# Even frequency classes of a real DFT transformed by row parity over half the columns, and the second batch's class sums moved into layer 1

## The chip, the cores and the metric

The kernel runs on one core of one Trainium2 chip. The metric is the device time of one execution in microseconds, the median of three runs. TensorE does the matrix products into PSUM, VectorE (DVE), ScalarE (ACT) and GpSimd (POOL) work elementwise, and SyncE (SP) issues most of the DMA transfers. Each engine runs its own instructions strictly in the order in which the program emits them.

## What is computed

```python
def _attn_ref(x):                      # x: 2 x 3008 x 256, float32
    X = np.fft.fft(x, axis=1)
    X = np.fft.fft(X, axis=2)
    return X.real.astype(np.float32)

def _moe_ref(x, w_in, w_out):          # 6016 tokens, 256 -> 2048 -> 256
    h = x @ w_in
    g = np.where(h >= 1, h, np.where(h <= -1, 0.0, (h + 1) ** 2 / 4.0))
    return g @ w_out

def _moe2_ref(x, w_in, w_out):
    h = x @ w_in
    g = np.maximum(0.01 * h, h)
    return g @ w_out
```

The second layer's input is the first layer's output, whose input is the real part of the two-dimensional transform.

## The kernel before

The rows of the sequence are folded by their symmetries, so that each batch becomes four classes of frequencies of 376 positions: class 0 holds the frequencies 4i (378 columns with its two ends), class 1 holds 4i + 2, and classes 2 and 3 hold the odd ones. With two batches these are eight units, u = 4b + class. A folded batch comes in three chunks of 126 rows: chunk 0 has the even rows, chunk 1 the odd rows, and chunk 2 has 63 even rows on partitions 0 to 62 and 62 odd ones on partitions 64 to 125.

The head prepares all that layer 1 needs. `load_x`, `load_q`, `sum_x` and `add_x` bring and add the source terms, `fold_x b c` (VectorE) folds a chunk, and `col_copy` sets one column of it aside. `even_product b j c` multiplies chunk c by a cosine and a sine matrix (`me`, loaded by `load_me`), each over 378 or 376 columns, into two PSUM banks. `odd_product b tr c` uses parity: the even rows go to one bank and the odd rows to another (`parts`), ScalarE copies one bank out (`odd_copy`), and VectorE forms the sum and the difference of the two (`odd_sum`). Every class is then split into a high half in the reduced format fp32r (`even_high`, `odd_high`, ScalarE) and a low remainder (`even_low`, `odd_low`, VectorE; with `_g` on GpSimd), which land in `bt[u]`. The column set aside is transformed by `col_even` and spread over the partitions by `col_even_out` (ScalarE) into `ct[0]`, `ct[1]`, `ct[4]`, `ct[5]`; the odd units' `ct` go out to DRAM as a row and come back spread over all partitions (`col_row`, SP's queue). The transform over the 256 features is folded into the first weights: `w1_begin`, `w1_exponent` and `w1_join` turn the 64-bit weights to float32, `g_product j` multiplies them by the feature transform, `g_high` and `g_low` split the result. `w2_*` do the same conversion for the second weights. `fill` issues matmuls on a constant tile whose result is not used.

Layer 1 has 128 steps, n = 16u + f, one for each unit and each block of 128 hidden features. A step's first product is 6 matmuls into a pair of banks `p` (high by high, high by low, low by high for two parts), VectorE makes `aa` from `ct`, `g128` and `p` and then the two `h`, ScalarE makes `r` in three instructions, VectorE takes the maximum in the next step, two steps later ScalarE writes the high half `gh` and GpSimd the low half `gl`, and four steps later (`LAG`) TensorE accumulates into four banks `acc` with 12 matmuls. Pairs of banks are double-buffered, so step n + 2 waits for `h` of step n. The single banks (four) serve `g_product`, `col_even`, some of the class products and, until `g_last 1`, the bank `g128`; from step 4 on they are `acc`.

The order of the head is written out by hand in `ORDER`: each engine takes its part of the items in that order. Work that has time is planned into the steps: `plan_at(step, (offset, kind, function))` puts a job behind a step. Steps 0 and 1 stand in `ORDER`, the later ones in a loop. Layer 2 follows with another 128 steps. The tail of the order before:

```python
# open_steps, odd_low 1 0, step 0, g_rows 1, odd_product 1 1 0, w2_join 3, even_low 1 1, odd_product 1 1 1,
# odd_product 1 1 2, w2_high 3, w2_high 1, odd_copy 1 1, w2_high 2, w2_low_g 3, w2_low_g 1, odd_sum 1 1,
# w2_low_g 2, g_last 1, w2_high 0, odd_high 1 1, odd_low_g 1 1, step 1, col_row 1, w2_low 0
```

Of the kernel before, what the change touches and what calls it, by code (L numbers as in the profile page):

```python
# [60 lines left out]

def _dft_even():

    s = _rows().astype(np.float64)[:, :, None]
    ok = s >= 0
    i = np.arange(378)[None, None, :]
# [66 lines left out]
1, odd_product 0 0 1, odd_product 0 1 1, g_product 4, load_me 2, w1_join 3, g_product 3, sum_x 0 2, fold_x 0
2, g_low 2, g_high 4, g_high 3, w1_begin 0, fill 1, odd_product 0 0 2, g_low 3, col_copy 0 2, load_w1 6,
even_product 0 1 0, even_product 0 1 1, load_x 1 1, w1_begin 6, g_row 3, load_me 0, g_low 4, odd_product 0 1
2, w1_exponent 0, odd_copy 0 0, add_x 1 1, w1_begin 5, load_me 1, fold_x 1 0, load_x 1 2, w1_join 0,
w1_exponent 6, even_product 0 1 2, even_product 0 0 0, g_product 0, odd_copy 0 1, odd_sum 0 0, even_product
0 0 1, g_row 2, odd_sum 0 1, even_product 0 0 2, w1_exponent 5, w1_join 5, even_high 0 1, load_w2 0,
even_low 0 1, load_w2 1, w1_join 6, even_high 0 0, w2_begin 1, fold_x 1 1, col_copy 1 0, odd_product 1 0 0,
load_w1 7, g_product 5, g_product 6, g_high 6, load_w2 2, odd_product 1 0 1, even_low 0 0, add_x 1 2,  # L140
load_w2 3, fold_x 1 2, even_product 1 0 0, col_row 0, g_high 0, w1_begin 7, col_copy 1 2, g_low 0, odd_high
0 0, w2_begin 0, even_product 1 0 1, w1_exponent 7, col_copy 1 1, g_row 4, w1_join 7, w2_exponent 1,
odd_product 1 0 2, g_product 7, load_w2 4, g_row 0, even_product 1 0 2, w2_join 1, odd_copy 1 0, odd_sum 1
0, w2_begin 2, g_high 5, odd_low_g 0 0, even_high 1 0, even_product 1 1 0, w2_exponent 0, g_rows 0, w2_join
0, g_high 7, even_product 1 1 1, odd_high 0 1, w2_begin 3, g_low 5, odd_low 0 1, g_low 6, g_low 7,
w2_exponent 2, w2_join 2, col_even 1, w2_exponent 3, even_low 1 0, g_row 7, even_product 1 1 2, g_last 0,
col_even 0, odd_high 1 0, g_row 5, col_even_out 1, even_high 1 1, g_row 6, col_even_out 0, open_steps,
# [8 lines left out]
def fnet_moe_kernel(ctx: ExitStack, tc: tile.TileContext, xpq, dft_e, dft_o, dft_d, pick,  # L156
# [146 lines left out]
    wpb = t5 = ta = th = None  # L303

    with tc.manual_schedule():
# [5 lines left out]
        ev = pool("ev", 4, late, "right")  # L311
# [11 lines left out]
        col = mo_p.tile([CH, 3, 2, B, P // B], F32, name="col")  # L323
# [22 lines left out]
        def load_me(j):  # L346
            me[j] = me_p.tile([P, 3, 378], F32, name=f"me{j}")
# [85 lines left out]
        def col_copy(b, c):  # L433
# [4 lines left out]
            A.copy(col[:, c, :, b, :], tc_[:, 0:2, P:P + 1].to_broadcast([CH, 2, P // B]))  # L438

        def both(c, j, lo=0, hi=CH):  # L440
            return col[lo:hi, c, j].rearrange("p b r -> p (b r)")

        def new_unit(u):
            bt[u] = by.tile([P, 4, 378], FR, tag="by", name=f"bt{u}")

        def even_parts(b, j):
            u = 4 * b + j
            n = 378 if j == 0 else H4
            return [(bt[u][:m, 2 * i, :n], bt[u][:m, 2 * i + 1, :n], p[:m, :n])
                    for i, (m, p) in enumerate(zip((P, 127), pde[b, j]))]  # L450

        def even_product(b, j, c):

            n = 378 if j == 0 else H4
            if c == 0:
                new_unit(4 * b + j)
                if (b, j) == (0, 1):
                    pde[b, j] = (psum_one(f"dc{b}{j}"), psum_one(f"ds{b}{j}"))
                else:
                    p = psum_pair(f"de{b}{j}")  # L460
                    pde[b, j] = (p[:, 0], p[:, 1])
            pc, pn = pde[b, j]
            tc_, ts_ = xt[b, c]
            T.matmul(pc[:, :n], lhsT=tc_[:, j, 0:P], rhs=me[2 * j][:CH, c, :n], start=(c == 0), stop=(c == 2))  # L464
            T.matmul(pn[:127, :n], lhsT=ts_[:, j, 0:127], rhs=me[2 * j + 1][:CH, c, :n], start=(c == 0), stop=(c == 2))

        def even_high(b, j):
            for hi, _, p in even_parts(b, j):
                A.copy(hi, p)

        def even_low(b, j):
            for hi, lo, p in even_parts(b, j):
                V.tensor_tensor(out=lo, in0=p, in1=hi.bitcast(F32), op=ALU.subtract)

        def col_even(j):
            n = 378 if j == 0 else H4
            pde["c", j] = p = psum_one(f"cc{j}")
            for c in range(3):
                T.matmul(p[:, :n], lhsT=both(c, j), rhs=me[2 * j][:CH, c, :n], start=(c == 0), stop=(c == 2))  # L479

        def col_spread(b, u, src):

            n = 378 if u == 0 else H4
            ct[4 * b + u] = t = cp.tile([P, 378], F32, tag="ct", name=f"ct{4 * b + u}")
            for h in range(2):
                A.copy(t[64 * h:64 * h + 64, :n], src[64 * b:64 * b + 64, :n])

# [447 lines left out]
```

## Time and profile before

| | |
|---|---|
| median of three runs (lowest to highest) | 981.23 us (980.51 to 981.66) |
| the profiled execution's own time | 983.23 us |
| its span in the profile | 978.4 us |
| TensorE, matmuls | 963.2 us busy, 5442 records |
| VectorE | 603.9 us |
| ScalarE | 707.9 us |
| GpSimd | 492.1 us |

The span is what the profiler records from the first to the last instruction; the execution's time holds also what lies around it. A matrix product in full float32 leaves two matmul records, one in fp32r leaves one. Busy times are those of one profiled execution; matmuls are pipelined, so the distance from one start to the next says more than a record's own duration.

### The profile page before, as it was taken

To read this page: it belongs to the slowest core of one execution; us is meant where nothing else is said; L and a number is where in the kernel's file an instruction comes from. 1 tells how busy PE (TensorE), PEld (TensorE's weight loads), DVE (VectorE), ACT (ScalarE), POOL (GpSimd) and SP (SyncE) were. 2 spreads that over 40 slices of the span, in tenths; PEclk is the share of its full clock that TensorE was granted. 3 is DMA by queue.
4 is the path that set the end of the run, shared out by engine and by line. 5 is a ranking of instruction groups with operands and counts; after the bars stand their busy time and mean duration, and the time that the engine had idled before them with its cause. 6 is when DMAs were issued, how large, how long until landed. Compare 5 with 4: busy or idle time off the path is not lost.

```text
span 978.4 us, 14606 instructions
## 1 busy us (share of the span) xinstructions
PE 963.2 (98%) x5442; PEld 937.0 (96%) x5442; DVE 603.9 (62%) x1005; ACT 707.9 (72%) x1236; POOL 492.1 (50%) x293
## 2 busy tenths in 40 slices
PE   8998999999999999999999999999999999999998
PEld 6558999999999999999999999999999999999998
DVE  6989988888798888887766473342433524325211
ACT  3488988878798888888766676666666666666654
POOL 0145655556556565656320455645646446465443
PEclk9998999999999999999999999999999999999999
DMA  9822010111010101011453210101001010000000
GB/s 353 295 68 74 1 54 12 54 43 54 12 54 33 64 12 54 11 65 44 141 203 119 85 44 16 48 1 64 1 16 49 1 64 1 1 32 1 33 1 31
DMA packets 19838, 56.47 MB, mean 58 GB/s; under 512 B 2564, under 2 KB 3128, under 8 KB 19640
## 3 DMA queue, kind: packets, MB, share of 16 engines
q1 hardware_dynamic: 18872, 53.56, 15.2%
q0 software_dynamic: 752, 1.61, 0.8%
q8 instruction: 42, 0.69, 0.3%
q10 hardware_dynamic: 144, 0.39, 0.1%
q14 instruction: 28, 0.23, 0.1%
HBM read 37.95 MB, written 14.44 MB: 54 GB/s over the span
## 4 chain that ended last, share of the span: by engine, by line
PE 91%; DVE 2%; ACT 2%; POOL 0%; issue 0%; ACTq 0%; DVEq 0%
PE acc L606 53%; PE p L589 13%; PE x L595 12%; PE v L595 6%; PE q L776 3%; PE y L595 3%; ACT gh L611 0%; PE do L499 0%; PE cc L479 0%; DVE aa L734 0%; ACT r L740 0%; ACT r L751 0%; DVE h L737 0%; DVE r L747 0%; PE de L464 0%; POOL gl L615 0%
## 5 line engine op out<-in xcount | busy, mean ns | idle before, releaser
L615 POOL TENSOR_TENSOR gl<-s,gh 128x752 fp32r<-128x752 f32 x113 | 205.6, 1820 | 240.1 <-ACT gh L611 239.3
L615 POOL TENSOR_TENSOR gl<-r,gh 128x752 fp32r<-128x752 f32 x128 | 239.2, 1869 | 164.7 <-ACT gh L611 136.8
L606 PE MATMUL acc<-gh,wd 128*128 128x376 f32 x1024 | 288.0, 334 | 0.4 <-DVE o L636 0.4
L606 PE MATMUL acc<-gh,wb 128*128 128x376 f32 x1024 | 282.2, 336 | 0.2
L606 PEld LDWEIGHTS acc<-gh,wb 128*128 128x128 f32 x1024 | 187.0, 189 | 3.3 <-ACT r L744 2.3
L606 PEld LDWEIGHTS acc<-gh,wd 128*128 128x128 f32 x1024 | 186.8, 188 | 0.7 <-DVE o L636 0.7
L606 PE MATMUL acc<-gl,wb 128*128 128x376 f32 x512 | 171.3, 335 | 1.2 <-POOL gl L615 1.2
L606 PE MATMUL acc<-gl,wd 128*128 128x376 f32 x512 | 170.1, 332 | 0.0
L589 PE MATMUL p<-bt,wa 127*128 127x376 f32 (+3 forms) x768 | 154.9, 337 | 4.5 <-DVE h L738 4.5
L763 ACT ACTIVATE s<-s 128x752 f32<-128x752 f32 x112 | 75.7, 676 | 94.2 <-DVE s L840 94.2
L589 PEld LDWEIGHTS p<-bt,wa 128*128 128x128 f32 (+1 forms) x768 | 135.4, 190 | 5.3 <-issue 5.1
L747 DVE TENSOR_TENSOR r<-h,r 128x752 f32<-128x752 f32 x128 | 125.6, 981 | 0.0
L830 DVE TENSOR_TENSOR s<-v,bb 128x376 f32<-128x376 f32 x56 | 30.8, 550 | 152.0 <-PE v L595 133.7
L611 ACT CAST gh<-s 128x752 fp32r<-128x752 f32 x128 | 105.2, 822 | 15.6 <-PE acc L606 10.9
L751 ACT ACTIVATE r<-r 128x752 f32<-128x752 f32 x128 | 106.8, 834 | 4.1
L740 ACT ACTIVATE r<-h 128x376 f32<-128x376 f32 x128 | 66.2, 517 | 59.7 <-DVE h L737 54.9
L734 DVE SCALAR_TENSOR_TENSOR aa<-ct,g,p 128x376 f32<-128x376 f32 (+1 forms) x128 | 77.3, 604 | 50.4 <-PE p L589 48.8
L611 ACT CAST gh<-r 128x752 fp32r<-128x752 f32 x128 | 103.3, 807 | 0.2 <-DVE r L747 0.2
L606 PEld LDWEIGHTS acc<-gl,wb 128*128 128x128 f32 x512 | 96.8, 189 | 2.3 <-POOL gl L615 2.3
L606 PEld LDWEIGHTS acc<-gl,wd 128*128 128x128 f32 x512 | 96.1, 188 | 0.0
L595 PE MATMUL x<-op,ws 128*128 128x376 f32 x336 | 76.0, 334 | 0.0
L595 PE MATMUL v<-op,ws 128*128 128x376 f32 x336 | 75.6, 333 | 0.0
(105 smaller groups left out, 1264.3 us busy)
## 6 DMA issues: line engine op xcount, KB each, us to landing
rw<-in_w_dram SPq DMA_DIRECT2D x32, 512.0 KB, 5.4
y<-o SPq DMA_DIRECT2D x16, 376.0 KB, 2.6
ry<-y SPq DMA_DIRECT2D x16, 376.0 KB, 3.6
out_dram<-o SPq DMA_DIRECT2D x15, 376.0 KB, 2.5
rf<-w3f SPq DMA_DIRECT2D x16, 256.0 KB, 2.7
x<-in_xpq_dram SPq DMA_DIRECT2D x6, 512.0 KB, 8.6
wt<-wc SPq DMA_DIRECT2D x8, 384.0 KB, 5.2
me<-in_dft_e_dram SPq DMA_DIRECT2D x4, 567.0 KB, 11.3
```

The costliest lines, as they stand in the source:

```text
L589: T.matmul(p[:, j, :n], lhsT=w[:m, 2 * j + x, :], rhs=b[:m, 2 * j + y, :n], start=(a == 0), stop=(a == 2))
L595: T.matmul(bank[:, :H4], lhsT=w[:, x, :], rhs=y[:, z, :], start=start and a == 0, stop=a == 2, skip_group_check=not start)
L606: T.matmul(acc[k][:, :H4], lhsT=w[:, x, m * P:(m + 1) * P], rhs=y[:, t, :], start=(f == 0 and i == 0), stop=(f == NF - 1 and i == 2))
L611: A.copy(gh[n], gp[n])
L615: engine.tensor_tensor(out=gl[n], in0=gp.pop(n), in1=gh[n].bitcast(F32), op=ALU.subtract)
L734: V.scalar_tensor_tensor(out=aa[:, :w], in0=ct[u][:, :w], scalar=g128[:, f:f + 1], in1=p[:, 0, :w], op0=ALU.mult, op1=ALU.add)
L740: A.activation(r[:, 0], h[:, 0], HOLD, scale=240.0)
L747: V.tensor_tensor(out=g, in0=hp.pop(n - 1), in1=g, op=ALU.max)
L751: A.activation(r, r, AF.Square, scale=0.5 / 240.0, bias=0.5)
L763: A.activation(out, h, AF.Prelu, alpha=0.01)
L776: T.matmul(p[:, t, :H4], lhsT=block[:, x, :], rhs=ops[0][d][:, t, z, :], start=(a == 0), stop=(a == 5))
L830: V.tensor_tensor(out=h1[:, 1], in0=v[:, :H4], in1=bb, op=ALU.add)
```

## The change

The even classes are transformed by parity like the odd ones. The matrices keep 192 columns instead of 378. `halves` sends even rows to one bank and odd rows to the other, cosine and sine part side by side in a bank; `even_copy` takes the even rows' bank out, and the sum and the difference of the two (`even_plus`, `even_minus`, 189 or 188 columns) give the two halves of the columns, which now lie in another order (`_even_columns`, undone on the host). The high and low halves are then taken from SBUF instead of PSUM. For batch 1, both banks of the even and of the odd classes are copied ("parked") into a tile, and sums, highs and lows are done by planned jobs in steps 18 to 58. The column set aside is transformed as one row a batch, its halves are combined on two partitions (`even_row`, `even_row_sum`), and it goes out to DRAM and comes back spread over the partitions (`even_row_out`, SP's queue). Steps 0 to 3 now stand in `ORDER`, whose items are put in a new order; the planned jobs of steps 0 to 3 are emitted behind it.

```diff
-        col = mo_p.tile([CH, 3, 2, B, P // B], F32, name="col")
+        col = mo_p.tile([CH, 3, 2, B], F32, name="col")
...
-            me[j] = me_p.tile([P, 3, 378], F32, name=f"me{j}")
+            me[j] = me_p.tile([P, 3, HW], F32, name=f"me{j}")
...
-            A.copy(col[:, c, :, b, :], tc_[:, 0:2, P:P + 1].to_broadcast([CH, 2, P // B]))
+            A.copy(col[:, c, :, b], tc_[:, 0:2, P])
...
+        parts = (((0, 0, CH),), ((1, 0, CH),), ((0, 0, 63), (1, 64, CH)))
+
+        def halves(banks, i, m, lhs, mat, c):
+            for par, lo, hi in parts[c]:
+                T.matmul(banks[par][:m, i * HW:(i + 1) * HW], lhsT=lhs(lo, hi), rhs=mat[lo:hi, c, :],
+                         start=(c == par and i == 0), stop=(c == 2), skip_group_check=(i > 0))
...
-            pc, pn = pde[b, j]
-            tc_, ts_ = xt[b, c]
-            T.matmul(pc[:, :n], lhsT=tc_[:, j, 0:P], rhs=me[2 * j][:CH, c, :n], start=(c == 0), stop=(c == 2))
-            T.matmul(pn[:127, :n], lhsT=ts_[:, j, 0:127], rhs=me[2 * j + 1][:CH, c, :n], start=(c == 0), stop=(c == 2))
+                pde[b, j] = two_banks(f"de{b}{j}", (b, j) == (0, 1))
+            for i, (x, m) in enumerate(zip(xt[b, c], (P, 127))):
+                halves(pde[b, j], i, m, lambda lo, hi: x[lo:hi, j, 0:m], me[2 * j + i], c)
+
+        def even_copy(b, j):
+            t = park("even")[:, 2 * j:2 * j + 2] if b else first_part(b, f"e{j}")
+            for i, m in enumerate((P, 127)):
+                for par in range(1 + b):
+                    A.copy(t[:m, i, par * HW:(par + 1) * HW], pde[b, j][par][:m, i * HW:(i + 1) * HW])
...
+        def even_plus(b, j, i):
+            m, e, o = sum_parts(b, j, i)
+            a = 189 - j
+            V.tensor_tensor(out=sum_tile(4 * b + j, i)[:m, :a], in0=o[:, :a], in1=e[:, :a], op=ALU.add)
+
+        def even_minus(b, j, i):
+            m, e, o = sum_parts(b, j, i)
+            a, k = 189 - j, 2 - 2 * j
+            x, y = (o, e) if i else (e, o)
+            V.tensor_tensor(out=ss[4 * b + j, i][:m, a:2 * a], in0=x[:, k:k + a], in1=y[:, k:k + a],
+                            op=ALU.subtract)
...
-            for h in range(2):
-                A.copy(t[64 * h:64 * h + 64, :n], src[64 * b:64 * b + 64, :n])
...
+            A.copy(e, p[0][:B, :HW])
+
+            def rest():
+                V.tensor_tensor(out=d[:, :a], in0=p[1][:B, :a], in1=e[:, :a], op=ALU.add)
+                V.tensor_tensor(out=d[:, a:z], in0=e[:, lo:hi], in1=p[1][:B, lo:hi], op=ALU.subtract)
...
+            nc.sync.dma_start(out=row[:, :z], in_=d[:, :z])
             for b in range(B):
...
+                nc.sync.dma_start(out=t[:, :z], in_=row[b:b + 1, :z].to_broadcast([P, z]))
...
         def odd_copy(b, tr):
-            pdo[b, tr] = sums_of_odd(f"{b}{tr}", pdo[b, tr], P)
+
+            if b:
+                for h in range(2):
+                    A.copy(park("odd")[:, 2 * tr + h, :H4], pdo[b, tr][h][:, :H4])
+            else:
+                A.copy(first_part(b, f"o{tr}").rearrange("p i n -> p (i n)")[:, :H4], pdo[b, tr][0][:, :H4])
...
+        at = 18
+        for u in (4, 5):
+            for i in range(2):
+                n, m = (378, H4)[u - 4], (P, 127)[i]
+                plan_at(at, (0, "V", lambda u=u, i=i: even_plus(1, u - 4, i)),
+                        (2, "V", lambda u=u, i=i: even_minus(1, u - 4, i)),
+                        (3, "A", lambda u=u, i=i, m=m, n=n: high_of(u, i, m, n)),
+                        (4, "V", lambda u=u, i=i, m=m, n=n: low_of(u, i, m, n)))
+                at += 6
+        for tr in range(2):
+            m = (P, 127)[tr]
+            plan_at(at, (0, "V", lambda tr=tr: odd_plus(1, tr)), (2, "V", lambda tr=tr: odd_minus(1, tr)))
+            if tr:
+                plan_at(at, (4, "S", lambda: col_row(1)))
+            for h in range(2):
+                plan_at(at, (3 + h, "A", lambda h=h, tr=tr, m=m: high_of(6 + h, tr, m, H4)),
+                        (5 + 2 * h, "V", lambda h=h, tr=tr, m=m: low_of(6 + h, tr, m, H4)))
+            at += 10
...
-            if 1 < n < N1 + 2:
+            if first_steps <= n < N1 + 2:
```

The weight tiles `wpb` are in two pools of four instead of one of eight, and the pool `t3` of `gh` and `gl` is opened by `open_steps`. The new order from the last fold on:

```python
# fold_x 1 2, odd_product 1 0 1, load_w2 2, even_product 1 0 2, g_low 5, w1_begin 7, col_copy 1 1, col_copy 1 2,
# odd_high 0 1, col_even 1, g_low 6, odd_product 1 0 2, w1_exponent 7, load_w2 0, w1_join 7, col_even 0, even_row 1,
# even_product 1 1 0, g_product 7, odd_product 1 1 0, even_row_sum 1, even_row_out 1, odd_copy 1 0, w2_begin 3,
# w2_join 1, even_low_g 0 1, g_low 0, even_row 0, g_row 0, even_product 1 1 1, w2_exponent 3, w2_begin 2, g_row 2,
# g_high 7, w2_begin 0, even_product 1 1 2, even_row_sum 0, w2_join 3, even_copy 1 0, even_low 0 0,
# odd_product 1 1 1, g_low 7, w2_exponent 2, odd_product 1 1 2, even_row_out 0, g_rows 0, w2_join 2, w2_exponent 0,
# g_row 5, open_steps, w2_high 3, w2_join 0, w2_high 1, w2_high 2, odd_low 0 0, g_row 7, g_row 6, w2_low_g 2,
# odd_low 0 1, g_last 0, load_w2 4, even_copy 1 1, w2_low 1, g_rows 1, w2_high 0, odd_copy 1 1, col_row 0, step 0,
# step 1, w2_low_g 0, step 2, step 3, g_last 1, w2_low 3
```

## Rows read from the trace of the kernel before

**Rows 1.** The page, part 1: busy time, share of the span and instructions of each engine.

```profile
PE 963.2 (98%) x5442; PEld 937.0 (96%) x5442; DVE 603.9 (62%) x1005; ACT 707.9 (72%) x1236; POOL 492.1 (50%) x293
```

**Rows 2.** Stretches: us, busy of PE, PEld, DVE, ACT, POOL, PEclk, DMA share, GB/s.

```profile
5.79:48.70 42.91, 40.98 (x162) 28.55 (x161) 38.15 (x94) 19.52 (x51) 4.99 (x7) 1.00 0.94 337
48.70:64.14 15.44, 14.86 (x56) 9.09 (x55) 12.92 (x27) 12.70 (x32) 4.91 (x8) 1.00 0.30 95
...
70.00:80.00 10.00, 5.28 (x20) 4.21 (x19) 9.90 (x17) 7.94 (x15) 6.21 (x6) 0.72 0.52 185
98.00:148.00 50.00, 49.95 (x290) 49.52 (x289) 45.07 (x74) 44.09 (x74) 30.24 (x16) 1.00 0.08 27
148.00:198.00 50.00, 49.98 (x290) 49.53 (x289) 41.38 (x69) 41.59 (x69) 29.48 (x16) 1.00 0.09 32
```

**Rows 3.** Timeline of TensorE in the head: start us, us, instruction, records.

```profile
31.49 1.54 PE L499 MATMUL do<-mo,xt 63*128 63x376 f32 x8
32.97 0.90 PE L464 MATMUL dc<-me,xt 126*128 126x376 f32 x2
...
36.44 1.89 PE L372 MATMUL g<-cw,cd 128*128 128x256 f32 x8
38.16 0.80 PE L464 MATMUL de<-me,xt 126*128 126x378 f32 x2
38.80 0.80 PE L465 MATMUL de<-me,xt 126*127 126x378 f32 x2
```

**Rows 4.** The chain that ended last, in order of time: start us, us, what.

```profile
57.41 1.90 PE cc L479 x6
...
62.99 1.05 PE p L589 x6
64.04 4.04 PE do L499 x16
...
68.10 0.62 ACT wb L293
...
68.74 0.48 ACT es L516
...
70.32 0.53 DVE aa L734
...
73.33 1.38 DVE wb L297
...
77.15 2.00 POOL gl L615
...
79.19 3.06 PE acc L606 x11
```

**Rows 5.** Timeline of VectorE in the head: start us, us, instruction, idle before.

```profile
27.14 2.07 DVE L395 TENSOR_TENSOR wa<-g,wa 128x256 fp32r<-128x256 f32 x6
...
48.70 0.75 DVE L395 TENSOR_TENSOR wa<-g,wa 128x256 fp32r<-128x256 f32 x2
...
50.48 2.33 DVE L216 TENSOR_SCALAR tw<-tw 128x512 int32<-128x512 int32 x1
...
59.48 0.42 DVE L216 TENSOR_SCALAR tw<-tw 128x512 int32<-128x512 int32 x1
59.93 0.69 DVE L221 SCALAR_TENSOR_TENSOR cw<-rw,tw 128x512 int32<-128x512 int32 x1
...
64.14 0.61 DVE L734 SCALAR_TENSOR_TENSOR aa<-ct,g,p 128x378 f32<-128x378 f32 x1 [1.28 <-ACT ct L486]
```

**Rows 6.** Timeline of GpSimd beside the stretched shift.

```profile
50.57 1.94 POOL L543 TENSOR_TENSOR bt<-bs,bt 128x376 fp32r<-128x376 f32 x2
```

**Rows 7.** Timeline of SP's queue: a row written out and read back.

```profile
51.02 0.33 SPq L556 DMA_DIRECT2D row<-bs  x1
53.96 0.35 SPq L558 DMA_DIRECT2D ct<-row  x1
```

**Rows 8.** Groups of VectorE's instructions from 98 to 498 us: busy us, mean ns.

```profile
L747 DVE TENSOR_TENSOR r<-h,r 128x752 f32<-128x752 f32 x120 | 116.8, 974 | 0.0
```

More of the change, by code (lines that the diff above doesn't have):

```diff
@@ L133 @@
[L133 to L147, printed above, removed]
@@ L148 @@
-odd_low 1 0, step 0, g_rows 1, odd_product 1 1 0, w2_join 3, even_low 1 1, odd_product 1 1 1, odd_product 1
-1 2, w2_high 3, w2_high 1, odd_copy 1 1, w2_high 2, w2_low_g 3, w2_low_g 1, odd_sum 1 1, w2_low_g 2, g_last
-1, w2_high 0, odd_high 1 1, odd_low_g 1 1, step 1, col_row 1, w2_low 0
+load_q 0 0, load_x 0 0, load_w1 2, w1_begin 2, load_w1 1, sum_x 0 0, load_x 0 2, load_cd, w1_begin 1, load_q
+0 2, fold_x 0 0, load_w1 4, load_w1 3, load_q 0 1, w1_begin 3, load_w1 0, w1_exponent 2, w1_exponent 1,
@@ new lines @@
+even_product 0 1 0, g_low 3, g_high 4, load_w1 5, odd_product 0 1 1, fold_x 1 0, g_low 1, load_x 1 2,
+even_product 0 1 1, add_x 1 2, w1_begin 5, w1_exponent 6, odd_product 0 1 2, w1_join 6, load_me 0, g_low 4,
+w1_exponent 5, odd_copy 0 0, load_w2 1, load_w2 3, even_product 0 1 2, odd_sum 0 0, even_copy 0 1, w1_join
+0, g_row 3, g_row 1, g_product 6, col_copy 1 0, even_sum 0 1, even_product 0 0 0, odd_high 0 0, odd_copy 0
+1, w2_begin 1, even_product 0 0 1, even_product 0 0 2, fold_x 1 1, even_high 0 1, load_w1 7, g_product 0,
@@ new lines @@
+w1_join 5, g_product 5, even_copy 0 0, w2_exponent 1, g_high 0, g_high 5, odd_sum 0 1, even_sum 0 0, g_row
+4, odd_product 1 0 0, g_high 6, even_high 0 0, even_product 1 0 0, even_product 1 0 1, fold_x 1 2,
+odd_product 1 0 1, load_w2 2, even_product 1 0 2, g_low 5, w1_begin 7, col_copy 1 1, col_copy 1 2, odd_high
+0 1, col_even 1, g_low 6, odd_product 1 0 2, w1_exponent 7, load_w2 0, w1_join 7, col_even 0, even_row 1,
+even_product 1 1 0, g_product 7, odd_product 1 1 0, even_row_sum 1, even_row_out 1, odd_copy 1 0, w2_begin
@@ new lines @@
+3, w2_join 1, even_low_g 0 1, g_low 0, even_row 0, g_row 0, even_product 1 1 1, w2_exponent 3, w2_begin 2,
+g_row 2, g_high 7, w2_begin 0, even_product 1 1 2, even_row_sum 0, w2_join 3, even_copy 1 0, even_low 0 0,
+odd_product 1 1 1, g_low 7, w2_exponent 2, odd_product 1 1 2, even_row_out 0, g_rows 0, w2_join 2,
+w2_exponent 0, g_row 5, open_steps, w2_high 3, w2_join 0, w2_high 1, w2_high 2, odd_low 0 0, g_row 7, g_row
+6, w2_low_g 2, odd_low 0 1, g_last 0, load_w2 4, even_copy 1 1, w2_low 1, g_rows 1, w2_high 0, odd_copy 1 1,
@@ L151 @@
+col_row 0, step 0, step 1, w2_low_g 0, step 2, step 3, g_last 1, w2_low 3
 """.replace("\n", " ").split(",")]
@@ L852, in layer_2_pair @@
             todo(n + 1, "V")
+        first_steps = sum(item.startswith("step") for item in ORDER)
         for item in ORDER:
             name, *args = item.split()
[L856 removed]
+            if name == "w2_high" and not wpb:
                 folded.close()
[L858 removed]
+                wpb.append(pool("wpb0", 4))
             if name == "step":
```

190 lines of the change are left out of this document (109 added, 81 removed).

## The prediction

> **What bounds the kernel now.** I read the page's engine shares first: TensorE is busy for 963 of the 978 us [rows 1], so a gain needs TensorE work taken away or its idle time filled. The table by stretches says where either is possible: from 98 us on it is busy without a gap [rows 2], and the change takes nothing away there. What can move is the head, up to the first accumulation of layer 1 at 79.19 us, from where the chain of waits stays on TensorE [rows 4]. In the head two engines are near full. Between 5.79 and 48.70 us TensorE shows 40.98 of 42.91 us and VectorE 38.15; between 48.70 and 64.14 TensorE shows 14.86 of 15.44 [rows 2], and the chain lies on it: column product, first step, odd product [rows 4]. The ramp of the pipeline behind that is VectorE's: 9.90 of 10 us in 70:80, with TensorE at 5.28 [rows 2].
>
> **What TensorE loses.** An even product now has 6 matmuls of 376 or 378 columns. Each is two records and takes 0.64 us (38.16 to 38.80 [rows 3]), 3.82 for one class of a batch. After: 4 matmuls over all rows of a chunk and 4 over half of them, 192 columns each. Eight 256-column records take 1.72 us (36.44 to 38.16 [rows 3]), 0.215 each, and a 378-column one 0.32: time goes with the columns, so 0.161 for 192, at most 0.215 if the proportion ends below 256. Eight full-row records: 1.29 (to 1.72). The half-row form stands in the odd product: eight 63-row records of 376 columns take 1.48 us (31.49 to 32.97 [rows 3]), 0.185 each. In proportion that is 0.76, without shortening 1.48; I take the middle, 1.1. A class costs 2.4 us (2.05 to 3.2) and four classes save 5.7 (2.5 to 7.1). A column product of 1.90 us [rows 4] becomes four records of 0.161 and four half-row ones, 1.2 us; two save 1.4 (1.0 to 1.8). Four more `fill` calls (25 for 21, counted in the order; two 256-column records each) are 1.7 us, but stand where TensorE waits for data; without that cover they come off the gain. Net 5 to 7 us less for TensorE ahead of the first accumulation.
>
> Four whole 376-column records would be 1.27 us; the eight half-row ones take 0.2 more than that [rows 3]. The Trainium skill (TensorEngine Tiling (Array Packing), Tiling Modes) says that a change of tiling mode drains the engine, which speaks against six such blocks more. Were the 0.2 that drain, fixed per block, with the halves side by side, a new block would be 4 x 0.161 + 0.2 = 0.85 and the sum 1 us better than mine; no block of other width in the trace decides it.
>
> **What VectorE gains and loses.** Its 256-wide subtractions take 0.345 us (six in 2.07 [rows 5]); a 189-wide operation lies between that and 189/256 of it, 0.255: I take 0.27, and 0.46 for a 376-wide one. Ahead of step 0's `aa`, `odd_sum 1 0`, `even_low 1 0`, `odd_low 1 0` (0.92 each) are gone, and `even_low 0 1` goes to GpSimd (0.92): -3.7. New are `odd_low 0 0` back from GpSimd (0.92), two `even_sum` (8 x 0.27 = 2.1), two `even_row_sum` (1.1), `w2_join 3` (0.69 [rows 5]) and `w2_low 1` (0.7): +5.5. So 1.8 us more work ahead of that `aa`, which is at 64.14 now [rows 5]. Behind it, before the first accumulation, `even_low 1 1`, `odd_sum 1 1`, `w2_join 3` and `w2_low 0` (1.38 [rows 4]) are gone, 3.9 us. VectorE as a whole has about as much to do, in another order; it gains only by waiting less. It waited 4.8 us before 48.70 and 2.5 from there to 64.14 [rows 2], and one shift took 2.33 us for the usual 0.42 while GpSimd subtracted [rows 5, 6].
>
> ScalarE loses eight column copies and gets two `even_row` copies, the parking copies and a longer `odd_copy`; at 12.70 of 15.44 us [rows 2] it has room, except just before step 0 (below). The four matrices of the even classes shrink by 378/192, from 567 to 288 KB each by their shape; 1.1 MB at 337 GB/s [rows 2] is 3 us of the load phase. That is cover under which the last rows come in time, not gain by itself.
>
> **Walking the new order.** The last `fold_x` ends at 48.70 now [rows 5]. Work ahead of it changes by two `even_sum` for two `even_low` and one exponent, +0.7; of 4.8 us waiting the loads allow perhaps 2 to go: 47.3 (44.6 to 49.4). Behind it TensorE has the rest of `even_product 1 0` (1.1), two column products (2.4), `odd_product 1 0 2` (1.48), `even_product 1 1` (2.4), `g_product 7` (1.72), `odd_product 1 1` (4.04 [rows 4]) and `g_last 0` (0.3): 13.4 us, so step 0 begins at 60.7, against 62.99 [rows 4], and `aa` at 61.8. VectorE has from 47.3 four `g_low` (2.8), four exponents (1.7), five joins (3.5), the row sums (1.1), three lows (2.8) and `w2_low 1` (0.7), 12.6 us, so 59.9, and up to 1.9 beside GpSimd. The even coefficient rows `ct` now go out to DRAM and back on SP's queue. For such a row the trace shows 2.94 us from the issue of the write to that of the read (51.02 to 53.96 [rows 7]); as much again for the read makes 6 to 7 with the issues. Behind the waiting write in SP's queue stand `load_w2 4` and `col_row 0`, whose rows are first needed 32 steps on. I place `even_row_sum 0` near 54, so `ct` lands near 61. Three strands meet at 61 to 62; for crossing waits (the two banks that `odd_product 1 1` gets only after `even_row_sum 0`, the `w2_high 1` that waits for its end) I take `aa` at 62.5.
>
> From step 1's `aa` (70.32) to the first accumulation (79.19) took 8.9 us with a `w2_low` of 1.38 in it [rows 4]. Now steps 0 to 3 run one after the other, step 1 some 1.6 us behind step 0. ScalarE has behind the end of `odd_product 1 1` still three `w2_high` (0.62 each), four 192-wide copies (about 0.3) and two 376-wide (0.48 [rows 4]), 4 us, and comes to step 0 about 1 us late. So 62.5 + 1.6 + 8.9 - 1.4 + 1.0 = 72.6, which is 6.6 us earlier.
>
> **Layer 1.** Parking moves 20 VectorE operations and 8 highs into steps 18 to 58: 12 for even classes (4.0 us) and 8 for odd ones (3.7). VectorE idles 8.6 of 50 us there, 0.54 a step [rows 2], 25 us over 46 steps. Between 98 and 148 us it ran at 45.07 of 50, denser than this will be, and TensorE stayed at 49.95 [rows 2]. I cost it at nothing; without that cover it would be the 7.7 us themselves. The wider tiles, the two weight pools and the earlier opened buffers add no instruction.
>
> **Sum.** Profiled span 978.4 - 6.5 = 971.9; that execution's own time, 983.23, is 2.0 above the median of the three runs, 981.23. The forecast is 981.2 - 6.5 = 974.7, in its own range 972.5 to 976.7.
>
> **Rivals.** *VectorE sets the head.* If its waiting stays, `aa` comes at 64.1 + 1.8 = 65.9 and the first accumulation near 76: gain 3, 978. For it: 1.8 us more work. Against: it waited for TensorE and loads.
>
> *TensorE's clock stays up in the ramp.* Now it is granted 0.72 in 70:80 [rows 2], and the first eleven accumulations take 3.06 us [rows 4], 1.2 more than at the 0.172 each of a later stretch (49.98 over 290 [rows 2]). With a shorter ramp and no start at 1.2 GHz, 1 to 3 more are gained: 972. Against: steps 0 to 3 have no odd product between them as cover. The Trainium skill (TensorE: Matmul & The Clock Gate, Part 1) calls the half rate the idle state; the granted 0.72 agrees.
>
> *No change.* The ramp without cover gives the saving back: `aa` of step 0 would have to come at 69, by waits of 7 us for banks or for the `ct` rows; 980 to 983.
>
> *Slower.* The parked sums have both operands in SBUF, where one was in PSUM. If GpSimd's `gl` (2.00 us [rows 4], GpSimd busy for 30.24 of 50 [rows 2]) shuts each out, 20 x 1.9 = 38 us of VectorE delay meets 25 of idle time: some 13 reach TensorE, less the 6.5: 988. It decides from about 1.6 us a piece. For it: the stretched shift [rows 5]. Against: `r`, also with two SBUF operands, averages 974 ns over 120 in layer 1, beside the same `gl` [rows 8], and two operations of half its width would take 0.92. The Trainium skill (SBUF — State Buffer, section SBUF: two separate sides) states such an exclusive lock between a VectorE operation with two SBUF inputs and one of GpSimd; by the 974 ns it costs little here.
>
> **Chances.** Forecast 0.5; clock stays up 0.12; VectorE sets the head 0.21; no change 0.09; slower 0.08. Faster by over 0.2% (2 us, about what a measurement of this kernel can tell) then holds 0.82, same 0.09, slower 0.09, with a little for the unnamed. The range 970.5 to 979.5 takes in the first three but for their tails.
>
> **What would show it.** In the profile after: even products of about 2.4 us; the last fold near 47; step 0's `aa` near 62.5, not waiting for `ct`; the first accumulation at 72 to 73; TensorE at 49.9 of 50 us in layer 1. The forecast is wrong if `aa` waits for SP's rows, if `odd_product 1 1` waits for banks for more than some 2 us, or if new TensorE gaps show between 130 and 260 us.

## The result, and the profile after

The changed kernel takes 990.0 us (989.38 to 991.41, four runs) against 980.95 us for the kernel before: 1.0094 of it, with a 95% interval of [1.0076, 1.0111]. It is 9 us slower where I forecast 6.5 faster. The profiled execution spans 989.6 us, 11.2 more than the one before. The page of the kernel after, parts 1 and 4 (busy time of each engine; share of the chain that ended last), and then part 4 of the page before:

```profile
PE 963.4 (97%) x5470; PEld 937.3 (95%) x5470; DVE 624.7 (63%) x1028; ACT 706.2 (71%) x1244; POOL 489.4 (49%) x290
...
PE 79%; DVE 13%; ACT 3%; issue 1%; DMA 1%; POOL 0%; DVEq 0%; ACTq 0%; POOLq 0%
```

```profile
PE 91%; DVE 2%; ACT 2%; POOL 0%; issue 0%; ACTq 0%; DVEq 0%
```

TensorE shows the same 963 us as before [rows 1], so 11 more of the span are idle, and 13% of the chain, for 2% before, now lies on VectorE. The stretches of the kernel after say where (columns as in [rows 2]):

```profile
70.00:80.00 10.00, 8.00 (x44) 7.16 (x43) 9.84 (x16) 7.21 (x12) 3.71 (x2) 1.00 0.44 161
98.00:148.00 50.00, 47.30 (x272) 46.36 (x271) 48.00 (x75) 41.83 (x71) 30.03 (x16) 1.00 0.08 27
148.00:198.00 50.00, 48.35 (x276) 47.05 (x275) 47.38 (x73) 40.57 (x69) 27.73 (x15) 1.00 0.09 32
198.00:298.00 100.00, 94.60 (x531) 92.30 (x530) 86.93 (x136) 78.15 (x131) 55.00 (x30) 0.98 0.13 44
42.00:46.00 4.00, 2.62 (x9) 2.22 (x10) 4.00 (x13) 0.08 (x2) 0.00 (x0) 0.83 0.40 122
46.00:50.00 4.00, 4.00 (x14) 2.75 (x14) 3.93 (x13) 3.97 (x15) 0.00 (x0) 0.74 0.03 12
```

The ramp is denser, 8.00 us of TensorE in 70:80 for the 5.28 of [rows 2]. But between 98 and 298 us, where before TensorE had 49.95 and 49.98 of 50 [rows 2], it now shows 47.30, 48.35 and 94.60 of 100. The last two lines are a gap in the head and its clock, to which I come below.

One mark in each step gives the account: the start of its `aa` on VectorE. The numbers are rows of VectorE's timeline.

| start of `aa`, us | step 0 | step 4 | step 18 | step 30 | step 40 | step 58 | step 127 |
|---|---|---|---|---|---|---|---|
| before | 64.14 | 80.47 | 123.68 | 161.26 | 192.62 | 249.51 | 467.03 |
| after | 66.46 | 78.89 | 122.93 | 162.71 | 195.87 | 259.50 | 477.14 |
| after less before | +2.3 | -1.6 | -0.75 | +1.45 | +3.25 | +10.0 | +10.1 |

So two things went wrong. Of the 6.5 us that the head should give, 0.75 is left at step 18. And between steps 18 and 58, just where the parked jobs stand and which I costed at nothing, 10.7 us are lost. From there on the kernels run alike (+0.1 to step 127, and 1.1 more of the span behind it).

The prices of the head were right. TensorE's timeline of the kernel after (start us, us, instruction, records, idle before):

```profile
34.55 0.82 PE L474 MATMUL de<-me,xt 63*128 63x192 f32 x8
35.30 1.99 PE L383 MATMUL g<-cw,cd 128*128 128x256 f32 x8
...
37.13 2.32 PE L474 MATMUL de<-me,xt 126*128 126x192 f32 x16
39.38 0.92 PE L383 MATMUL g<-cw,cd 128*128 128x256 f32 x3
...
43.38 2.56 PE L383 MATMUL g<-cw,cd 128*128 128x256 f32 x8 [2.01 <-DVE cw L230]
...
51.67 1.23 PE L474 MATMUL cc<-me,col 126*2 126x192 f32 x8
52.84 0.59 PE L572 MATMUL do<-mo,xt 63*128 63x376 f32 x2
...
54.31 1.23 PE L474 MATMUL cc<-me,col 126*2 126x192 f32 x8
...
64.80 0.38 PE L394 MATMUL g<-pk,gr 16*128 16x8 f32 x2 [0.98 <-DMA gr<-rows]
```

A whole even class, its eight full-row and eight half-row records, takes 2.25 us from start to start (forecast 2.4), a column product 1.17 (forecast 1.2).

What happens between steps 18 and 58 is seen when VectorE's timeline is laid beside GpSimd's. First VectorE, then GpSimd, of the kernel after:

```profile
118.31 2.30 DVE L306 TENSOR_TENSOR wb<-cw,wb 128x512 fp32r<-128x512 f32 x1
...
123.56 0.55 DVE L828 TENSOR_TENSOR h<-aa,p 128x376 f32<-128x376 f32 x1
...
124.48 1.29 DVE L838 TENSOR_TENSOR r<-h,r 128x752 f32<-128x752 f32 x1
125.69 1.96 DVE L509 TENSOR_TENSOR bs<-even 128x189 f32<-128x189 f32 x1
...
132.44 0.93 DVE L838 TENSOR_TENSOR r<-h,r 128x752 f32<-128x752 f32 x1
133.29 0.35 DVE L515 TENSOR_TENSOR bs<-even 128x189 f32<-128x189 f32 x1
...
204.51 0.54 DVE L598 TENSOR_TENSOR bs<-odd 128x376 f32<-128x376 f32 x1
204.97 2.30 DVE L230 SCALAR_TENSOR_TENSOR cw<-rw,tw 128x512 int32<-128x512 int32 x1
207.19 0.59 DVE L825 SCALAR_TENSOR_TENSOR aa<-ct,g,p 128x376 f32<-128x376 f32 x1
```

```profile
118.17 1.88 POOL L688 TENSOR_TENSOR gl<-r,gh 128x752 fp32r<-128x752 f32 x1 [0.58 <-ACT gh L684]
...
123.15 1.82 POOL L688 TENSOR_TENSOR gl<-r,gh 128x752 fp32r<-128x752 f32 x1 [3.10 <-ACT gh L684]
125.56 1.89 POOL L688 TENSOR_TENSOR gl<-r,gh 128x752 fp32r<-128x752 f32 x1 [0.58 <-POOL gl L688]
...
133.53 1.82 POOL L688 TENSOR_TENSOR gl<-r,gh 128x752 fp32r<-128x752 f32 x1 [1.52 <-ACT gh L684]
...
204.74 1.98 POOL L688 TENSOR_TENSOR gl<-r,gh 128x752 fp32r<-128x752 f32 x1 [1.31 <-ACT gh L684]
```

The same operation on 189 columns takes 0.35 us at 133.29 and 1.96 us at 125.69. At 133.29 GpSimd's `gl` starts 0.24 us after it; at 125.69 `gl` has started 0.13 us ahead, and VectorE's operation ends only behind the end of `gl` (127.65 and 127.45). I went through all parked sums and lows and all weight conversions from 100 to 270 us: each one that `gl` was ahead of (by 0.04 to 0.23 us) took 1.96 to 2.34 us, each that started 0.14 us or more ahead of it, or with no `gl` about, 0.34 to 0.68. Eight were shut out: five of the 20 parked operations, and three conversions (118.31, 152.33, 204.97). The first of these stands ahead of step 18, so seven fall into steps 18 to 58; together they lasted 11.4 us longer than such operations do unhindered. In the kernel before none of the seven conversions `wb` and `cw` in the same stretch is shut out: each starts ahead of its `gl`, by 0.14 to 0.57 us, the one that answers to 204.97 by 0.23 (VectorE, then GpSimd):

```profile
201.23 0.68 DVE L221 SCALAR_TENSOR_TENSOR cw<-rw,tw 128x512 int32<-128x512 int32 x1
```

```profile
201.46 2.13 POOL L615 TENSOR_TENSOR gl<-r,gh 128x752 fp32r<-128x752 f32 x1 [1.30 <-ACT gh L611]
```

Two ways lead into the loss, both in the rows above. At 204.97 the conversion is the second job of its step, behind a parked sum, and so late by that sum's 0.46 us. At 125.69 VectorE is a little behind: its maximum `r` ran under the previous `gl` (1.29 us instead of 0.93), `gl` follows 0.58 us behind the last one, and the job behind `r` comes too late. Each time a conversion is the first to be shut out: 118.31 ahead of 125.69, 152.33 ahead of 165.39 and 172.46, 204.97 ahead of 212.36 and 231.10. The one at 118.31 has no parked job ahead of it: VectorE came to it late from the ramp, as the experiment on the ramp shows.

A step with a shut-out job lasts 5.10 us on VectorE (`aa` at 202.09 to 207.19), where TensorE needs 3.13 us a step (63 steps of the kernel before from 269.70 to 467.03). VectorE then runs its steps back to back in 2.40 us (207.19 to 209.59) until it has caught up. What TensorE waits for meanwhile, from 123 to 260 us (total us, times, longest), and then the same of the kernel before from 123.68 to 249.51:

```profile
PE acc L679 <- DVE o L709: 5.5, 3, 2.4
PE acc L679 <- POOL gl L688: 3.3, 5, 1.5
PE p L662 <- DVE h L829: 0.5, 1, 0.5
```

```profile
PE acc L606 <- POOL gl L615: 0.5, 1, 0.5
```

More than half falls at the ends of units, where VectorE copies two of the four banks `acc` out to SBUF (`o`) before they can be filled again; that copy stands in VectorE's queue behind the late steps. Most of the rest is `gl`, which comes late. These 9.3 us, for 0.5 before, are most of the 10.7. Behind one of the gaps, 1.96 us long, the clock was 0.83 in 238:248, which is the 0.98 of the stretches above: at most 1.7 us more, by my estimate (0.17 of 10 us).

The kind of operands matters as well. `h` reads one operand from PSUM. From 100 to 300 us 96 of its 120 instructions start while GpSimd is at work, as at 123.56 under the `gl` of 123.15, and every one of the 120 takes 0.54 or 0.55 us.

The Trainium skill (SBUF — State Buffer, section SBUF: two separate sides) says of the port pair that VectorE and GpSimd share that whichever starts first holds it for the whole instruction; the trace agrees, in either direction: 1.96 instead of 0.35 us for VectorE, 2.13 instead of 1.82 for `gl` at 201.46.

### The profile page after: what moved, and what is told of

The parts are those of the page before. It is cut to its first block, busy times and chain, and to the rows that moved or that the text cites. A ratio compares the mean times of both kernels' runs of the same rounds, so it can differ in the third digit from the quotient of the medians.

```text
span 989.6 us, 14713 instructions
## 1 busy us (share of the span) xinstructions
PE 963.4 (97%) x5470; PEld 937.3 (95%) x5470; DVE 624.7 (63%) x1028; ACT 706.2 (71%) x1244; POOL 489.4 (49%) x290
## 4 chain that ended last, share of the span: by engine, by line
PE 79%; DVE 13%; ACT 3%; issue 1%; DMA 1%; POOL 0%; DVEq 0%; ACTq 0%; POOLq 0%
PE acc L679 46%; PE x L668 12%; PE p L662 9%; PE v L668 6%; DVE r L838 3%; PE q L867 3%; PE y L668 3%; DVE aa L825 2%; DVE h L829 1%; DVE h L828 1%; DVE cw L230 1%; ACT gh L684 1%; ACT r L842 1%; DVE xt L423 1%; PE do L572 1%
## 5 line engine op out<-in xcount | busy, mean ns | idle before, releaser
L838 DVE TENSOR_TENSOR r<-h,r 128x752 f32<-128x752 f32 x128 | 128.2, 1002 | 0.8 <-ACT r L842 0.8
```

What stands on the lines that cost most here:

```text
L838: V.tensor_tensor(out=g, in0=hp.pop(n - 1), in1=g, op=ALU.max)
```

## Experiments

Four theories were on the table. A: the parked operations, with both operands in SBUF, meet `gl` and are shut out. B: VectorE simply has more to do in these steps. C: the head hands over a pipeline that is behind, and the loss is its late start. D: TensorE's granted clock. For these steps the stretches above leave D little: 1.00 to 198 us, and the 0.83 in 238:248 stands behind a gap that the late steps made. The ratios are to the kernel before on the same chip.

**No parked jobs.**

```diff
-        at = 18
-        for u in (4, 5):
...
-            at += 10
...
-        sx = pool("sx", 2, parts_p)
+        for u in range(4):
+            bt[4 + u] = bt[u]
+        for u in (2, 3):
+            ct[4 + u] = ct[u]
```

> Leaves out the planned sums, highs and lows of batch 1 in steps 18 to 58; batch 1's units read batch 0's tiles and rows instead, so the second batch's result is that of the first. Theory A (lock): the parked VectorE operations have two SBUF operands and wait for GpSimd's gl; the 11 us of TensorE idle between 100 and 300 us are those waits: 977 to 979. Theory B (load): VectorE simply has 7.7 us more to do there: the same, 977 to 979. Theory C (late start): VectorE enters layer 1 behind because of what is piled up at steps 0 to 8, and that delay is carried on: 987 to 990.

978.65 us, 0.9982 [0.9972, 0.9992]. From step 18 to step 58 it takes 125.70 us, before 125.83, after 136.57. The loss needs the parked jobs, as A or B have it; the late start (C), which this kernel has too, does not cost it alone.

**The same operations ahead of the maximum.** The 20 operations are the same; they only stand in front of the previous step's `r` instead of behind it.

```diff
+            todo(n, "P")
             gp[n - 1] = g = rp.pop(n - 1)
...
-                plan_at(at, (0, "V", lambda u=u, i=i: even_plus(1, u - 4, i)),
-                        (2, "V", lambda u=u, i=i: even_minus(1, u - 4, i)),
+                plan_at(at, (0, "P", lambda u=u, i=i: even_plus(1, u - 4, i)),
+                        (2, "P", lambda u=u, i=i: even_minus(1, u - 4, i)),
...
-                        (4, "V", lambda u=u, i=i, m=m, n=n: low_of(u, i, m, n)))
+                        (4, "P", lambda u=u, i=i, m=m, n=n: low_of(u, i, m, n)))
...
```

> The same parked VectorE operations, each put ahead of the maximum of its step instead of behind it, so that it begins before GpSimd's gl of that step. A: the operations take 0.35 and 0.54 us instead of up to 2.2, TensorE stays busy, 977 to 982. B: VectorE has the same work, 988 to 991. C: 987 to 990.

980.99 us, 1.0003 [0.9993, 1.0013]. Groups of VectorE's instructions from 98 to 300 us, of the kernel after and then of this one (busy us, mean ns):

```profile
L838 DVE TENSOR_TENSOR r<-h,r 128x752 f32<-128x752 f32 x61 | 63.1, 1034 | 0.0
...
L529 DVE TENSOR_TENSOR bt<-bs,bt 128x376 fp32r<-128x376 f32 x3 | 3.3, 1085 | 0.0
```

```profile
L230 DVE SCALAR_TENSOR_TENSOR cw<-rw,tw 128x512 int32<-128x512 int32 x4 | 6.0, 1500 | 0.0
...
L529 DVE TENSOR_TENSOR bt<-bs,bt 128x376 fp32r<-128x376 f32 x3 | 2.0, 651 | 0.0
```

With the same work in another order steps 18 to 58 take 128.08 us, 8.5 less than after: A and not B. What is left, 2.25 over before, goes with the conversions, which here still stand behind the maximum: in these steps two of them are shut out (`cw`, 1500 ns on the mean of four), and a third ahead of step 18. The other 2.4 us between the two profiled spans are the head's, and they go with the clock: this one was granted 1.00 where the kernel after had 0.83 and 0.74:

```profile
42.00:46.00 4.00, 2.67 (x11) 2.19 (x12) 4.00 (x13) 0.64 (x3) 0.00 (x0) 1.00 0.44 145
46.00:50.00 4.00, 4.00 (x23) 2.75 (x22) 3.93 (x13) 3.96 (x15) 0.00 (x0) 1.00 0.03 10
```

The head is the same in both kernels, and so is the gap ahead of the fall (2.62 and 2.67 of 4 us busy); step 0's `aa` comes at 64.05 here and at 66.46 after. TensorE's timeline of this kernel:

```profile
52.94 1.23 PE L474 MATMUL cc<-me,col 126*2 126x192 f32 x8
...
62.38 0.38 PE L394 MATMUL g<-pk,gr 16*128 16x8 f32 x2
```

The second column product starts 1.4 us ahead of the 54.31 of after; that much TensorE lost at the low clock. The other 1.0 us is the wait of `g_last 0` for its gathered rows (0.98 us at 64.80 after), which this execution doesn't have.

**The same operations on GpSimd.** Every function of the sums and lows gets its engine as an argument, for example:

```diff
-        def even_plus(b, j, i):
+        def even_plus(b, j, i, V=V):
...
-                plan_at(at, (0, "V", lambda u=u, i=i: even_plus(1, u - 4, i)),
+                plan_at(at, (0, "V", lambda u=u, i=i: even_plus(1, u - 4, i, G)),
```

> The 20 parked operations on GpSimd instead of VectorE, behind gl in its queue. A: no lock between the two, and GpSimd has some 1.2 us idle a step for 0.5 to 1.0 us of work: 976 to 981. B: VectorE is relieved of the load: 976 to 981. C: 987 to 990. If gl is pushed back so far that accumulations wait, above 985.

982.95 us, 1.0022 [1.0012, 1.0031], above what A had named. The meeting is not avoided, it only changes sides; now the maximum waits for GpSimd (group of VectorE from 98 to 300 us):

```profile
L838 DVE TENSOR_TENSOR r<-h,r 128x752 f32<-128x752 f32 x63 | 74.8, 1187 | 0.1
```

That is 0.15 us more in each of 63 steps than after's 1034, and 0.20 more than before's 985 in the same stretch. Yet steps 18 to 58 take 127.97 us, no more than with the sums ahead of the maximum (128.08). Of the 4.0 us between these two profiled spans 2.65 lie ahead of step 0, where this execution had the low clock in 42:50, and 1.4 behind step 58, where a conversion is shut out (254.18, 2.30 us).

**The ramp put in order.** The planned jobs of steps 0 to 3 stood behind all four steps, so `w2_low 3` (2.22 us, at 75.58 under a `gl`) and a conversion came in one block ahead of step 4. Here each step's jobs follow it, and the low goes to GpSimd.

```diff
-# col_row 0, step 0, step 1, w2_low_g 0, step 2, step 3, g_last 1, w2_low 3
+# col_row 0, step 0, step 1, w2_low_g 0, w2_low_g 3, step 2, step 3, g_last 1
...
+                todo(int(*args))
...
-            todo(n)
+            if n >= first_steps:
+                todo(n)
```

> Only the ramp is changed: the planned jobs of steps 0 to 3 are emitted behind their own steps instead of all ahead of step 4, and w2_low 3 goes from VectorE (2.22 us there, beside gl) to GpSimd ahead of its first gl. A: the 2 to 3 us lost between the first accumulation and step 8 come back, the waits of the parked operations stay: 986 to 988. B: the same, 986 to 988. C: VectorE enters layer 1 on time and the stalls there go too: 975 to 979.

986.0 us, 1.0048 [1.0033, 1.0063]. Stretches of this kernel:

```profile
98.00:148.00 50.00, 49.97 (x290) 49.53 (x289) 45.43 (x77) 43.88 (x74) 31.00 (x17) 1.00 0.08 27
148.00:198.00 50.00, 48.32 (x276) 47.01 (x275) 47.94 (x75) 40.22 (x68) 28.32 (x16) 1.00 0.10 32
198.00:298.00 100.00, 94.62 (x540) 92.32 (x539) 88.36 (x139) 80.24 (x134) 55.28 (x30) 1.00 0.13 44
```

To 148 us TensorE is full, as before. Behind that the holes are those of the kernel after, 48.32 and 94.62, so C is not the cause of them. But it is not without effect. The conversion at 118.31 and the sum at 125.69 are not shut out here (0.68 at 118.12 and 0.35 at 124.35), and steps 18 to 58 take 133.44 us, 3.1 less than after and 7.6 more than before. Step 0 to step 18 takes 55.48 us for 56.47. So of the 10.7 us some 3 need the late start and the parked jobs together, and 1.0 us is the ramp's own.

**Ramp and order together.**

> Both earlier edits together: the parked operations ahead of the maximum, the planned jobs of steps 0 to 3 behind their own steps, and w2_low 3 on GpSimd. If the two losses are separate (waits for gl in steps 18 to 58, 9 us by the first edit; pile at steps 4 to 8, 4 us by the second), they add: 976 to 978. If the pile of the ramp is only a part of the same delay, nothing is added: 980 to 982.

982.18 us, 1.0004 [0.9994, 1.0014], with both edits above. In the medians the two do not add up, and why stays open: the twelve times lie in two groups, 978.5 to 980.8 (four) and 982.1 to 983.2 (eight). The profiled execution (978.49, span 976.7, clock 1.00 in 42:50) is of the lower one. In the profiles they do: against the kernel with the order alone, also at 1.00 there, step 0 to step 18 takes 54.39 us for 56.47, steps 18 to 58 take 128.19 for 128.08, and the span is 2.0 us shorter.

**The kernel before with the meetings added.** Twenty subtractions of two SBUF tiles whose result is not used, behind the maximum in the same steps and of the same widths; head and all else are the kernel before.

```diff
+        def extra(n):
+            V.tensor_tensor(out=dm[:, :n], in0=bt[4][:, 0, :n].bitcast(F32), in1=bt[4][:, 1, :n].bitcast(F32),
+                            op=ALU.subtract)
+
+        at = 18
+        for n in (378, 378, H4, H4):
+            plan_at(at, *((x, "V", lambda w=w: extra(w)) for x, w in ((0, n // 2), (2, n // 2), (4, n))))
+            at += 6
...
```

> The kernel before, with 20 more VectorE subtractions of two SBUF operands (8 of 189 or 188 columns, 12 of 376 or 378) at the same places of steps 18 to 58, behind the maximum; their results are not used, the output is the reference's. Theory A: the place behind the maximum is enough, they wait for gl as the parked ones do: 985 to 991. Theory A with a condition (only a VectorE that is already late meets gl): they slip in ahead of gl, 981 to 983. Theory B: 7.7 us of work in 25 us of idle, 981 to 983, but then the order within the step would not have mattered.

991.86 us, 1.0112 [1.0099, 1.0125]: the whole loss, without the change. VectorE and then GpSimd:

```profile
158.54 1.30 DVE L758 TENSOR_TENSOR r<-h,r 128x752 f32<-128x752 f32 x1
159.76 2.16 DVE L704 TENSOR_TENSOR dm<-bt 128x378 f32<-128x378 f32 x1
```

```profile
157.22 1.82 POOL L615 TENSOR_TENSOR gl<-r,gh 128x752 fp32r<-128x752 f32 x1 [3.10 <-ACT gh L611]
159.62 1.88 POOL L615 TENSOR_TENSOR gl<-r,gh 128x752 fp32r<-128x752 f32 x1 [0.59 <-POOL gl L615]
```

The same picture as at 125.69, in eight jobs (six of the 20, two `cw`). Steps 18 to 58 take 137.31 us, 11.5 more than before.

**All planned jobs ahead of the maximum, with the ramp in order.** The conversions move too:

```diff
-        return ([("S", lambda: c.load(w3, j)), ("A", c.begin), ("V", c.exponent), ("V", spill)],
+        return ([("S", lambda: c.load(w3, j)), ("A", c.begin), ("P", c.exponent), ("P", spill)],
...
-                    (7, "V", to_low))
+                    (7, "P", to_low))
```

> As the run before, and the other planned VectorE jobs with two SBUF operands in layer 1 (the lows of w2 4 to 7, the exponents and joins of w3) also ahead of the maximum. Theory A (the lock strikes whatever stands behind the maximum): the lows of 2.2 us and the joins of 2.3 fall to 0.7, another 1 to 2 us less than the run before, 975 to 977. If those waits meet idle time of VectorE: no change against it, 976 to 978.

977.73 us (976.27 to 978.92), 0.9967 [0.9955, 0.9979]: faster than both kernels. Its stretches in layer 1, and its group of the conversions from 98 to 300 us:

```profile
98.00:148.00 50.00, 49.97 (x289) 49.53 (x289) 45.19 (x77) 43.80 (x73) 30.59 (x17) 1.00 0.09 31
148.00:198.00 50.00, 49.98 (x290) 49.54 (x289) 43.94 (x76) 42.73 (x71) 30.18 (x17) 1.00 0.09 30
198.00:298.00 100.00, 98.22 (x565) 96.87 (x564) 86.36 (x144) 83.73 (x139) 59.62 (x32) 1.00 0.13 43
```

```profile
L230 DVE SCALAR_TENSOR_TENSOR cw<-rw,tw 128x512 int32<-128x512 int32 x5 | 3.4, 684 | 0.0
```

The longest of all these jobs is 0.86 us, and steps 18 to 58 take 126.75 us, 0.9 more than before.

**That order with the ramp of the change**, to price the ramp by itself.

> The changed kernel with all planned two-operand VectorE jobs of layer 1 ahead of the maximum, the ramp as in the change. If the ramp's pile costs 2 to 4 us of its own: 979.5 to 982. If the order within the step is all: 977 to 978.

979.93 us, 0.9979 [0.9967, 0.999]. The medians put the ramp of the change at 2.2 us, but these seven runs spread from 977.61 to 981.71, and the clock in the head is mixed up with it: the profiled execution here had 0.78 and 0.79 in 42:50, that of the better version 1.00. In the profiles step 0 to step 4 takes 12.44 us here and 10.37 with the ramp in order, but step 0 to step 18 55.08 and 54.04: 1.0 us of it remains.

**That order in the kernel before**, to see whether the gain is the change's or the order's (the two lines of the diff with the conversions, and `todo(n, "P")`, in the kernel before).

> The kernel before with its planned lows, exponents and joins of layer 1 ahead of the maximum. If the order within the step helps any kernel: 978 to 980. If the waits for gl there meet idle time of VectorE, as TensorE's 49.95 of 50 us say: 980.5 to 981.5, and what the best kernel gains comes from the head of the change.

981.32 us, 1.0001 [0.9993, 1.001]: the order alone gives the kernel before nothing, since none of its jobs was shut out. The 3.3 us of the better version come with the change's head and ramp. Its step 0 is not earlier (64.88 for 64.14), but its step 18 is, by 4.8 us (118.92 for 123.68): `odd_product 1 1`, which took 4.04 us between steps 0 and 1 [rows 4], is done ahead of step 0.

**TensorE's time given back.** Sixteen `fill` calls, 6.9 us of TensorE, behind the even and the column products: what TensorE saved is put back where it was saved, on top of the kernel with ramp and order together and again on top of the better version (977.73 us).

```diff
+            if c == 2:
+                fill(3)
...
+            fill(2)
```

> The first kernel of this set, with the TensorE time that the parity form saves in the head given back as idle products: 3 fill calls behind each even product, 2 behind each column product, 16 calls of 0.43 us. If TensorE sets the head, 5 to 7 us more than that kernel: 982 to 984. If VectorE and the transfers set it, at most 1 more: 976 to 979.

> The kernel of 977.7 us with 16 fill calls (6.9 us) given back to TensorE in the head, 3 behind each even product and 2 behind each column product. If TensorE sets the head: 982 to 985. If VectorE and the transfers set it: at most 979.

On the kernel with ramp and order together 983.73 us, 1.0029 [1.002, 1.0039]: 1.6 over it in the medians, of which its two groups allow no reading, and 5.8 in the profiled spans (982.5 and 976.7, both at clock 1.00 in the head). On the better version 982.07, 1.0006 [0.9998, 1.0015]: 4.3 over it, and 3.8 in the spans (979.6 and 975.8). So 55 to 84% of the 6.9 us, by the profiles, is on the path, and with it put back nothing of the 3.3 us is left.

**Fills in the ramp against half the clock.** In the better version the first accumulations still run at a low clock.

```diff
-# w2_low_g 3, step 2, step 3, g_last 1
+# w2_low_g 3, fill 2, step 2, fill 2, step 3, fill 3, g_last 1
```

> The fastest kernel so far (977.7, all planned jobs ahead of the maximum and the ramp spread) with seven fill calls between steps 1 to 3 of the ramp, while TensorE waits there. Theory D (the clock): TensorE idles in the ramp, is granted a lower clock (0.89 in 64 to 80 us) and pays 1 to 3 us for the first accumulations and more in some runs: 975 to 976.5, granted clock 0.999 or 1.0, runs closer together. If the fills are in the way of steps 2 and 3: 978 to 980. If the clock costs nothing there: 977.5.

978.76 us (975.55 to 982.39, twelve runs), 0.9975 [0.9961, 0.999]. Theory D is not borne out: no gain over 977.73. The median alone does not exclude it, since the runs spread over 7 us and the profiled execution was granted 0.65 in 42:46, so that its step 0 came at 66.29, 1.4 us behind the better version's 64.88. But behind step 0 the clock was up, 1.00 in 70:80 for 0.83 in the better version, and step 0 to step 18 took 54.63 us for 54.04: no gain there either.

## Why the prediction was wrong

**The step that failed is "Layer 1 … I cost it at nothing".** I set 7.7 us of operations against 25 us of idle VectorE, and took TensorE's 49.95 us in 98:148 beside a VectorE at 45.07 [rows 2] as proof that there is room. Idle time is no cover here: an operation that starts 0.1 us behind `gl` lasts 2 us, however much idle time its engine has. In layer 1 the sum was 10.7 us off (steps 18 to 58). The sign that I had named for it, new TensorE gaps between 130 and 260 us, is there. (The 25 us were 0.54 a step over 46 steps; steps 18 to 58 are 41, so 22. Either is far above 7.7.)

**The evidence against the rival was read wrongly.** I held the 974 ns of `r` [rows 8] against the lock, "beside the same `gl`". But `r` follows `h`, and ScalarE's `gh`, which releases `gl`, needs longer; so `r` starts about a microsecond ahead of its own `gl` and meets only the tail of the one before, 0.93 or 1.3 us. What stands behind `r` starts where `gl` starts. Not the kind of operands alone decides, but the place in the step. `h`, with one operand in PSUM, is not stretched once from 100 to 300 us. The rows that would have told me lie in the trace of before: `cw` at 201.23 with `gl` at 201.46 has a margin of 0.23 us, less than one more sum (0.35 or 0.54 us) takes.

**The rival "Slower" was what happened.** I priced it at 988 and measured 990.0. That its total came near is luck. Its working was 20 pieces of 1.9 us against 25 of idle time, less a gain of 6.5 in the head. What happened in steps 18 to 58 were seven pieces of some 1.6 us, two of them conversions that I had not counted, of which 10.7 us arrive at TensorE, and a gain of 0.75 ahead of them.

**The head gave 0.75 us at step 18 instead of 6.5.** The prices held. The other terms:
- Step 0's `aa` came at 66.46, not 62.5. The kernel with the sums ahead of the maximum, whose head is the same, had it at 64.05 at full clock: 2.4 of the 4.0 go with the low clock in 42:50, for which I had no term: 1.4 on TensorE itself, and 1.0 as the wait of `g_last 0` for the rows of its gather (0.98 us at 64.80), a chain that I had left out. Why that chain was later too is not shown. TensorE, with less to do, waited 2.01 us for `cw` at 43.38, and ran at half clock for a part of the time behind that. With fills put back into the better version it was busy for 4.00 of 4 us in 42:46, at 1.00.
- The other 1.6: the last fold ended at 49.2 for 47.3 (two pieces of a fold were stretched to 1.20 and 1.07 us beside `even_low_g` on GpSimd, at 39.73 for 2.23), and 49.1 with two such pieces in the kernel that had 64.05. From there to step 0's products TensorE took 13.6 us in that kernel, for the 13.4 of my sum. The `ct` rows by SP's queue, which I feared, were in time.
- From step 0 to step 18 the kernel gains 3.1 us (56.47 for 59.54) where I had 4.9. The missing 1.8 us fit the block of planned jobs ahead of step 4: in three pairs of profiles the ramp in order makes this stretch 1.0 (twice) and 2.1 us shorter.

**The rivals that did not decide.** VectorE does not set the head: putting TensorE's time back cost 3.8 to 5.8 of 6.9 us. The clock in the ramp did stay up, as that rival had it (1.00 in 70:80, for 0.72 in [rows 2]), but no gain from it can be seen: with the ramp in order, step 0 to step 18 took 54.39, 54.04 and 54.63 us in three executions that were granted 0.66, 0.83 and 1.00 in 70:80 (the last one with fills).

## What to carry to other kernels

Where VectorE and GpSimd both work from SBUF in one pipelined loop, the price of an added VectorE operation with both operands in SBUF is not its duration but its place: read from the trace when GpSimd's long operation starts, and put the new one where it surely starts first, ahead of the operation that waits for others. Look at the margins of the operations that are there already: a sum of 0.46 us put ahead of a conversion cost that 1.6 us. A mean duration proves nothing for another place in the same loop.

## Unexpected of the hardware

A margin of 0.2 us between two engines decides over 1.6 us: among the sums, lows and conversions of the kernel after, from 100 to 270 us, there was nothing between 0.68 and 1.96 us.

Work given to GpSimd to spare VectorE slows VectorE: the twenty operations there made `r` last 1187 ns on the mean, for 1034.

Less work for TensorE can make it slower for a while. The change leaves it a gap of 1.2 to 2.2 us in 42:46. Of nine profiled executions with this gap six had a low clock there and up to 50 us (0.83 and 0.74 in the kernel after), and their step 0 came at 66.3 to 66.7; three were granted 1.00, and theirs came at 63.9 to 64.9. The widest gap, 2.16 us, is among the three. With the gap filled, twice, the clock was 1.00. What decides is open.

The half-row blocks of 192 columns are cheap: eight records 0.75 us (34.55 to 35.30), in proportion to the 376-column form [rows 3]: the low end of my price for it (0.76), and not the middle (1.1).
